# Attention, an expert layer and a routed expert layer in one launch: the second product's last two token groups taken together, later weight splits kept behind the token list, and the places left compared on VectorE

## The chip, the cores and the metric

One core of one Trainium2 chip runs the whole program in one launch. The metric is the device time of that launch in microseconds (us), lower is better. Times of the kernel before are three runs; the trace is one further execution taken with the profiler.

## The reference

The program computes three layers, one behind the other, for 2304 tokens of width 512 (4 sequences of 576 tokens, 8 heads of 64):

```python
x = attention(q, k, v, f)                 # causal, with a decay from cumsum(log f)
h = x @ w_in                              # 512 -> 2048
x = np.maximum(0.01 * h, h) @ w_out       # 2048 -> 512
logits = x @ w_gate                       # 8 experts, cap = 288 tokens for each
for idx in np.argsort(-logits.flatten()): # best pair of token and expert first
    tok, e = idx // 8, idx % 8
    if assigned[tok] < 0 and counts[e] < cap:
        assigned[tok] = e; counts[e] += 1
for e in range(8):
    out[assigned == e] = np.maximum(x[assigned == e] @ w1[e], 0) @ w2[e]   # 512 -> 1024 -> 512
```

Weights of the first two layers come as 64-bit floats. All large products are made from a high and a low part of each operand (fp32r tiles `wh`, `gh`, `gl` and their like): three products for one.

## The kernel before, in words

Four stages follow each other. Attention and the first half of `h` come first, then the second half of `h` with the logits; both are ordered by a planner (`Plan`) that the change does not touch. The stage that the change touches comes next, and the routed experts last.

**The second product** (`x @ w_out`) is a generator, `deferred` (L989). It goes over 9 groups `g` of 256 tokens; for each over two halves of the 2048 inner columns (`half` 0 reads `g1`, which lies in SBUF, `half` 1 reads `gd` from DRAM through the tile `g0`), over four quads `i`, and two blocks `j` of 128 columns. `split_g` (L417) makes `gh` on ScalarE and `gl` on GpSimd. `second` (L425) issues 6 products of 128x512 into the two `acc` tiles of the group and yields behind each one: 96 products for a group, 864 in all. When a group is done, ScalarE copies `acc` to `xo` (two buffers), and SP stores it to `x2d` in DRAM, where the experts' tokens are gathered from.

**The token list** is another generator, `routing` (L1166). It runs 8 phases `ph`, one for each choice of a token that is still free. In 7 of them every expert with too many tokens finds the smallest key that it still takes, by two halves of three steps: VectorE compares all keys with 63 or 31 candidates (`ge`), TensorE counts for each expert and candidate (`q_ct`, 18 small products), VectorE finds how many candidates are exceeded by an expert (`found`), and TensorE turns that into the next `base`. Each count starts with a product of a row of ones (`of`) with minus the places left (`nr`), so that the comparison is with zero. Behind the six steps the counts of the key found go through `q_misc` (products with `on` and with `tru`), and VectorE makes the next phase's choice `oh` and adds the assigned tokens. Behind phase 8 comes the end of the list: a count with `tri`, the position of each token, the tiles `ga`, `oa` (half of it on GpSimd) and three tiles `ob`, 18 products into `q_misc`, and `ids`.

The two are woven by hand: `routing` yields a number of ns where TensorE would wait, and the loop at L1056 then issues products of `deferred` for it, one for each 216 ns of 1.62 times that number. `mm` (L1049) keeps TensorE's order as written. The other engines' orders are made by the tile scheduler from a simulated time, except for instructions issued through the wrappers `vec`, `act`, `gp`, `sp` (`InOrder`, L54), which keep the order of the program among themselves.

**Weights.** All split weights lie in 40 tiles under the tag `w`. In this stage 32 hold the two halves of `w_out` (`wo` and `wo0`, four tiles for each quad). `split_weights` (L317) loads 512 KB into one of two buffers `wst`, and makes two `wh` on ScalarE and two low parts on the engine that it is given: GpSimd for expert 0, VectorE for the others (`fetch`, L1071). Expert 0 takes 32 tiles, 8 of which are free early; the others come free as the last group is done with them.

**Experts.** For each expert, three gathers of 96 tokens on GpSimd (L1088), transposes (`turn`), two layers of products (`first`, `after`) and three scattered stores (`leave`). `fetch(e + 1)` and the gathers of expert `e + 1` are issued before expert `e`'s products.

Of the kernel before, what the change touches and what calls it, by code (L numbers as in the profile page):

```python
# [12 lines left out]
FT = mybir.dt.float32  # L13
FR = mybir.dt.float32r
BF = mybir.dt.bfloat16
I32 = mybir.dt.int32
AF = mybir.ActivationFunctionType
OP = mybir.AluOpType
# [4 lines left out]
E, F2 = 8, 1024  # L23
CAP = NTOK // E
NT = NTOK // 128
GT = 256
# [7 lines left out]
NF = 8  # L34
# [163 lines left out]
def tile_kernel(ctx, tc, q, k, v, f, w_in, w_out, w_gate, w1, w2, out):  # L198
# [218 lines left out]
    def split_g(g):  # L417

        gh = gtp.tile([128, 2, GT], FR, name="gh", tag="gh", bufs=3)
        gl = gtp.tile([128, 2, GT], FR, name="gl", tag="gl", bufs=3)  # L420
        A.copy(gh, g)  # L421
        G.tensor_tensor(gl, g, gh, op=OP.subtract)  # L422
        return gh, gl

    def second(mm, acc, gh, gl, wo, first, last):  # L425
        wh, wl = wo
        for t in range(GT // 128):
            s = slice(128 * t, 128 * t + 128)
            for n, (a, w) in enumerate(((gh, wh), (gh, wl), (gl, wh))):
                mm(acc[t], a[:, s], w, start=first and n == 0, stop=last and n == 2)  # L430
                yield True
# [555 lines left out]


    def deferred(ps, mm):  # L989
        for g in range(NG):  # L990
            acc = [psa.tile([128, 512], FT, name="acc", tag="acc", bufs=ACB) for _ in range(GT // 128)]
            for half in range(2):
                for i in range(NF // 2):
                    if half:
                        x = gtp.tile([128, 2, GT], FT, name="g0", tag="g0", bufs=3)
                        nc.sync.dma_start(x, gd[g][:, 2 * i:2 * i + 2])
                    else:
                        x = g1[g][:, 2 * i:2 * i + 2]
                    gh, gl = split_g(x)
                    for j in range(2):  # L1000
                        w = (wo0 if half else wo)[i]["w"][j]
                        yield from second(mm, acc, gh[:, j], gl[:, j], w, half == i == j == 0, half == j == 1 and i == NF // 2 - 1)
            for t in range(GT // 128):
                xo = gtp.tile([128, DM], FT, name="xo", tag="xo", bufs=2)
                A.copy(xo, acc[t])
                nc.sync.dma_start(x2d[GT * g + 128 * t:GT * g + 128 * t + 128], xo)

    with ExitStack() as c2:
        g1p = c2.enter_context(tc.tile_pool(name="g1", bufs=1, reuse_waits="tile"))
# [43 lines left out]
        wo0 += [{"w": split_weights([(0, 1024, wod[jj])], V)} for jj in range(NF // 4, NF // 2)]  # L1053
        rest = deferred(ps, mm)
        slack = 0
        for ns in routing(nc, rt, ids, ps, W0, mm):  # L1056
            slack += 1.62 * ns
            while slack > 108 and next(rest, None):
                slack -= 216
# [4 lines left out]
    with ExitStack() as c3:  # L1064
# [5 lines left out]

        def fetch(e):  # L1071

            lo_on = G if e == 0 else V
            wa = [[], []]
            for u in range(2):
                for c in range(0, NC, 2):
                    wa[u] += split_weights([(512 * i, 512 * i + 512, w1[e, 128 * (c + i):128 * (c + i) + 128, 512 * u:512 * u + 512])
                                            for i in range(2)], lo_on)
            wb = []
            for j in range(0, NJ, 2):  # L1080
                wb += split_weights([(512 * i, 512 * i + 512, w2[e, 128 * (j + i):128 * (j + i) + 128]) for i in range(2)], lo_on)
            return wa, wb
# [80 lines left out]
            leave(E - 1, ys, t)  # L1163


def routing(nc, wk, ids, ps, W0, mm):  # L1166

# [39 lines left out]
    G.affine_select(tri, on, pattern=[[1, 128]], base=0, channel_multiplier=-1, compare_op=OP.is_gt, fill=0.0)  # L1209
    tru = T("tru", 128, dt=BF)  # L1210
    V.tensor_tensor(tru, on, tri, op=OP.subtract)
    of = T("of", 64)
    G.memset(of, 1.0)
    seg = T("seg", E, NT)
    G.memset(seg, 1.0)
    G.memset(seg[:, :, 0:1], 0.0)
# [19 lines left out]
    for ph in range(E):  # L1236
# [24 lines left out]
        for half in range(2):  # L1261
            base = None
            for n, (K, kt, at0) in enumerate(steps):
                ct = Q("ct", 512, 2)[:, :E]
                mm(ct[:K], of[0:1, :K], nr[0:1], start=True, stop=False)
                ge = T("ge", NT, 63, dt=BF)
                s = [128, NT, K]
                V.scalar_tensor_tensor(ge[:, :, :K], key[:, :, None].to_broadcast(s), base if n else 0.0,
                                       kt[:, None, :].to_broadcast(s), op0=OP.subtract, op1=OP.is_ge)
                yield 500 + 19 * K  # L1270
                for i in range(NT):
                    mm(ct[:K], ge[:, i, :K], oh[:, :, i], start=False, stop=i == NT - 1)
                jk = T("jk", E, dt=BF)
                V.tensor_scalar(jk[at0:at0 + K], ct[:K], 0.0, -1.0, op0=OP.is_ge, op1=OP.max, accum_out=found[at0:at0 + K])
                base = Q("base", 512)[:, 0:1]
                yield 430
                mm(base, unit[:at0 + K], found[:at0 + K], start=True, stop=True)
            yield 480 * (half == 0)
            if half == 0:
                k3 = T("k3", NT)  # L1280
                V.tensor_scalar(k3, key, base, 131072.0, op0=OP.subtract, op1=OP.mult)
                V.tensor_tensor(k3, k3, kf[:, 1], op=OP.add)
                key = k3
# [72 lines left out]
            mm(p[:NB, :2 * NA], ob[:, i - i0, :], oa[:, i].rearrange("p a n -> p (a n)"), start=i == 0, stop=i == NT - 1)  # L1356
    idf = T("idf", NA)
    V.tensor_copy(idf[:NB], p[:NB, NA:2 * NA])
    V.scalar_tensor_tensor(ids, p[:NB, :NA], 128.0, idf[:NB], op0=OP.mult, op1=OP.add)


# [22 lines left out]
```

## Time and profile before

| what | value |
|---|---|
| median of 3 runs | 1039.38 us (1038.36 to 1041.74) |
| the profiled execution | 1040.22 us, its span 1038.5 us |
| mean granted clock of TensorE | 0.982 |
| busy: TensorE / VectorE / ScalarE / GpSimd | 981.7 / 613.5 / 457.3 / 439.4 us |
| second product and token list | about 521 to 798 us |
| experts | about 798 to 1038 us |

The span is from the first to the last instruction in the trace. A line's idle time is that of its engine just before it, with what ended it behind an arrow. A busy TensorE is not TensorE at its peak: products are pipelined, and a record's length overlaps the next record, so prices of products are better read from start to start.

### The profile page before, as it was taken

To read this page: it belongs to the slowest core of one execution; us is meant where nothing else is said; L and a number is where in the kernel's file an instruction comes from. 1 tells how busy PE (TensorE), PEld (TensorE's weight loads), DVE (VectorE), ACT (ScalarE), POOL (GpSimd) and SP (SyncE) were. 2 spreads that over 40 slices of the span, in tenths; PEclk is the share of its full clock that TensorE was granted. 3 is DMA by queue.
4 is the path that set the end of the run, shared out by engine and by line. 5 is a ranking of instruction groups with operands and counts; after the bars stand their busy time and mean duration, and the time that the engine had idled before them with its cause. 6 is when DMAs were issued, how large, how long until landed. Compare 5 with 4: busy or idle time off the path is not lost.

```text
span 1038.5 us, 20151 instructions
## 1 busy us (share of the span) xinstructions
PE 981.7 (95%) x7255; PEld 815.7 (79%) x7255; DVE 613.5 (59%) x1661; ACT 457.3 (44%) x1181; POOL 439.4 (42%) x558
## 2 busy tenths in 40 slices
PE   5999999999989999999999999999985999999996
PEld 3666666777579898889977777777764999999996
DVE  6798998666367787842444445434564565665541
ACT  5798888667523232332412222222141454555531
POOL 6266775322577776700154334444484111222011
PEclk9999999999989999999999999999996999999998
DMA  5577789574498855532221111121134456666521
GB/s 112 139 183 209 209 198 220 147 178 134 123 309 308 265 183 168 145 113 84 86 94 61 43 61 51 62 62 52 51 112 147 145 170 204 195 196 189 161 80 39
DMA packets 145061, 147.67 MB, mean 142 GB/s; under 512 B 70048, under 2 KB 99232, under 8 KB 144704
## 3 DMA queue, kind: packets, MB, share of 16 engines
q1 hardware_dynamic: 141888, 136.93, 45.5%
q0 software_dynamic: 3072, 9.44, 3.1%
q8 instruction: 57, 0.93, 0.4%
q14 instruction: 44, 0.36, 0.1%
HBM read 106.67 MB, written 30.65 MB: 132 GB/s over the span
## 4 chain that ended last, share of the span: by engine, by line
PE 73%; issue 9%; DVE 7%; DMA 5%; POOL 3%; ACT 2%; SPq 0%; POOLq 0%; DVEq 0%
PE acc L1050 20%; PE h L62 19%; PE h L1106 6%; PE y L1119 5%; PE T L62 5%; PE mx L62 5%; PE av L62 5%; PE st L62 3%; PE q_ct L1050 3%; DMA qb<-qa 2%; DMA wst<-in_moe_w 1%; DVE wbits L62 1%; POOL out L1127 1%; DVE kept L62 1%; ACT qa L62 1%
## 5 line engine op out<-in xcount | busy, mean ns | idle before, releaser
L62 PE MATMUL h<-X,wh 128*128 128x256 f32 x1728 | 237.8, 288 | 3.1 <-DVE g L62 3.0
L62 PEld LDWEIGHTS h<-X,wh 128*128 128x128 f32 x1728 | 215.8, 190 | 21.8 <-issue 14.5
L1050 PE MATMUL acc<-wh,gh 128*128 128x512 f32 x576 | 194.6, 406 | 0.0
L422 POOL TENSOR_TENSOR gl<-g,gh 128x512 fp32r<-128x512 f32 x72 | 96.8, 1346 | 128.2 <-ACT gh L421 116.6
L62 ACT ACTIVATE g<-h 128x256 f32<-128x256 f32 x144 | 55.3, 384 | 166.0 <-PE h L62 163.5
L1050 PEld LDWEIGHTS acc<-wh,gh 128*128 128x128 f32 x576 | 109.4, 191 | 20.8
L421 ACT CAST gh<-g 128x512 fp32r<-128x512 f32 x72 | 44.5, 620 | 174.5 <-PE acc L1050 155.4
L1106 PE MATMUL h<-XE,wh 128*128 128x288 f32 x768 | 119.4, 305 | 1.3 <-DVE el L1111 1.0
L1050 PE MATMUL acc<-wh,gl 128*128 128x512 f32 x288 | 119.1, 413 | 0.0
L325 ACT CAST wh<-wst 128x512 fp32r<-128x512 f32 x132 | 79.9, 620 | 85.8 <-DMA wst<-in_moe_w 55.7
L326 DVE TENSOR_TENSOR wh<-wst,wh 128x512 fp32r<-128x512 f32 x116 | 78.2, 688 | 61.7 <-ACT wh L325 53.9
L1106 PEld LDWEIGHTS h<-XE,wh 128*128 128x128 f32 x768 | 107.5, 192 | 2.1 <-DVE el L1111 1.5
L62 ACT ACTIVATE kept<-kept,nm 128x192 f32<-128x192 f32 (+2 forms) x192 | 97.8, 511 | 13.9 <-DVE nm L62 13.8
L62 DVE TENSOR_TENSOR g<-g,h 128x256 f32<-128x256 f32 x144 | 60.1, 417 | 70.4 <-ACT g L62 68.5
L1119 PE MATMUL y<-eh,wh 128*128 128x288 f32 x512 | 98.1, 296 | 0.0
L1119 PEld LDWEIGHTS y<-eh,wh 128*128 128x128 f32 x512 | 79.2, 188 | 0.4 <-ACT eh L1110 0.4
L1127 POOL DMA_INDIRECT out<-yo,ids x24 | 24.2, 1008 | 130.7 <-DVE yo L1126 123.4
L62 DVE CUSTOM_DVE_ANT_0 kept<-mx,mask 128x192 f32<-128x192 f32 (+4 forms) x160 | 63.9, 427 | 21.9 <-PE mx L62 18.0
L62 PE MATMUL mx<-ka,qa 128*128 128x192 f32 (+2 forms) x192 | 68.2, 362 | 5.3 <-DVE nm L62 4.5
L62 PE MATMUL av<-P,vt 128*64 128x256 f32 (+4 forms) x512 | 69.1, 356 | 1.7 <-DVE R L62 1.4
L62 ACT ACTIVATE P<-st 128x320 f32<-128x320 f32 (+2 forms) x128 | 62.9, 500 | 15.7 <-PE st L62 14.8
L62 DVE SCALAR_TENSOR_TENSOR wbits<-w,wbits 128x256 int32<-128x256 int32 x128 | 66.9, 524 | 2.1
(189 smaller groups left out, 1707.2 us busy)
## 6 DMA issues: line engine op xcount, KB each, us to landing
wst<-in_moe_w SPq DMA_DIRECT2D x128, 256.0 KB
X<-xd SPq DMA_DIRECT2D x10, 1024.0 KB
gd<-g SPq DMA_DIRECT2D x36, 256.0 KB
g<-gd SPq DMA_DIRECT2D x36, 256.0 KB
w<-in_moe_w_in SPq DMA_DIRECT2D x32, 256.0 KB
w<-in_moe_w_out SPq DMA_DIRECT2D x32, 256.0 KB
xd<-xt SPq DMA_DIRECT2D x16, 320.0 KB
R<-invd SPq DMA_DIRECT2D x32, 144.0 KB
```

What stands on the lines that cost most here:

```text
L62: r = getattr(self.engine, name)(*a, **k)
L325: A.copy(r[u][0], x)
L326: lo_on.tensor_tensor(r[u][1], x, r[u][0], op=OP.subtract)
L421: A.copy(gh, g)
L422: G.tensor_tensor(gl, g, gh, op=OP.subtract)
L1050: tc.keep_in_program_order(PE.matmul(*a, **k))
L1106: PE.matmul(h[:, :CAP], w, X[:, c, x, :], start=n == 0, stop=n == 3 * NC - 1)
L1119: PE.matmul(yt[c][:, :CAP], w[:, s], a, start=j == 0 and n == 0, stop=j == NJ - 1 and n == 2)
L1127: sd = G.indirect_dma_start(out=out[:, :], out_offset=bass.IndirectOffsetOnAxis(ap=ids[:, 3 * e + t:3 * e + t + 1], axis=0), in_=y, in_off ...
```

## The change

Three edits. In `deferred` groups 7 and 8 are one entry: for each half and quad, the 12 products of group 7 are followed by the 12 of group 8, into four `acc` tiles; their copies and stores come at the end. In `fetch` the low parts of experts 1 to 7, and in `routing` the last operation (`ids`), are issued through `vec`. In the list's steps the product of `of` and `nr` goes; a `tensor_tensor_reduce` adds `nr` to the counts and takes the maximum over the experts, and a comparison of that one column with zero gives `found`.

```diff
     def deferred(ps, mm):
-        for g in range(NG):
-            acc = [psa.tile([128, 512], FT, name="acc", tag="acc", bufs=ACB) for _ in range(GT // 128)]
+        for gs in [[g] for g in range(NG - 2)] + [[NG - 2, NG - 1]]:
+            acc = {g: [psa.tile([128, 512], FT, name="acc", tag="acc", bufs=ACB) for _ in range(GT // 128)] for g in gs}
             for half in range(2):
                 for i in range(NF // 2):
+                    for g in gs:
...
-            for t in range(GT // 128):
+            for g in gs:
+                for t in range(GT // 128):
...
-        for ns in routing(nc, rt, ids, ps, W0, mm):
+        for ns in routing(nc, rt, ids, ps, W0, mm, vec):
...
-            lo_on = G if e == 0 else V
+            lo_on = G if e == 0 else vec
...
-    of = T("of", 64)
-    G.memset(of, 1.0)
...
                 ct = Q("ct", 512, 2)[:, :E]
-                mm(ct[:K], of[0:1, :K], nr[0:1], start=True, stop=False)
...
-                    mm(ct[:K], ge[:, i, :K], oh[:, :, i], start=False, stop=i == NT - 1)
-                jk = T("jk", E, dt=BF)
-                V.tensor_scalar(jk[at0:at0 + K], ct[:K], 0.0, -1.0, op0=OP.is_ge, op1=OP.max, accum_out=found[at0:at0 + K])
+                    mm(ct[:K], ge[:, i, :K], oh[:, :, i], start=i == 0, stop=i == NT - 1)
+                jk, most = T("jk", E), T("most", 1)
+                V.tensor_tensor_reduce(out=jk[:K], in0=ct[:K], in1=nr[:K], scale=1.0, scalar=-3e38, op0=OP.add, op1=OP.max, accum_out=most[:K])
+                V.tensor_scalar(found[at0:at0 + K], most[:K], 0.0, None, op0=OP.is_ge)
...
-    V.scalar_tensor_tensor(ids, p[:NB, :NA], 128.0, idf[:NB], op0=OP.mult, op1=OP.add)
+    vec.scalar_tensor_tensor(ids, p[:NB, :NA], 128.0, idf[:NB], op0=OP.mult, op1=OP.add)
```

How instructions move. On TensorE, behind the first step of a half, before (`q_base` is the new base, `acc` the second product):

```order
L1050 MATMUL q_base<-r_found,r_unit 128x1
L1050 MATMUL q_ct<-r_nr,r_of 31x8
L1050 MATMUL acc<-wh,gl 128x512
L1050 MATMUL acc<-wh,gh 128x512 x2
L1050 MATMUL acc<-wh,gl 128x512
```

and with the change:

```order
L1053 MATMUL q_base<-r_found,r_unit 128x1
L1053 MATMUL acc<-wh,gl 128x512
L1053 MATMUL acc<-wh,gh 128x512 x2
L1053 MATMUL acc<-wh,gl 128x512
```

The product of `nr` and `of` is gone, and the products of the second layer close up.

On VectorE at the end of the list, before (`wh<-wst,wh` is the low part of a weight of expert 1; the T rows belong to the transposes of expert 0's tokens):

```order
L1345 TENSOR_TENSOR r_ga<-r_na,r_io 128x432
L1353 TENSOR_TENSOR r_ob<-r_nb,r_io 128x576
L1348 TENSOR_TENSOR r_oa<-r_ga,r_it 128x18x24
L326 TENSOR_TENSOR wh<-wst,wh 128x512 x2
L1353 TENSOR_TENSOR r_ob<-r_nb,r_io 128x576
L326 TENSOR_TENSOR wh<-wst,wh 128x512
L1353 TENSOR_TENSOR r_ob<-r_nb,r_io 128x576
L326 TENSOR_TENSOR wh<-wst,wh 128x512
L1358 COPY r_idf<-q_misc 96x24
L1359 SCALAR_TENSOR_TENSOR ids<-q_misc,r_idf 96x24
L1098 TENSOR_TENSOR XE<-T_9963,XE 128x288
```

and with the change:

```order
L1346 TENSOR_TENSOR r_ga<-r_na,r_io 128x432
L1354 TENSOR_TENSOR r_ob<-r_nb,r_io 128x576
L1349 TENSOR_TENSOR r_oa<-r_ga,r_it 128x18x24
L1354 TENSOR_TENSOR r_ob<-r_nb,r_io 128x576 x2
L1359 COPY r_idf<-q_misc 96x24
L62 SCALAR_TENSOR_TENSOR ids<-q_misc,r_idf 96x24
L1101 TENSOR_TENSOR XE<-T_10003,XE 128x288
L1101 TENSOR_TENSOR XE<-T_10009,XE 128x288
L1101 TENSOR_TENSOR XE<-T_10015,XE 128x288
L1101 TENSOR_TENSOR XE<-T_10021,XE 128x288
L62 TENSOR_TENSOR wh<-wst,wh 128x512 x4
```

The four splits stand behind `ids` and the four low parts of expert 0's tokens.

On GpSimd from the first weights of groups 7 and 8 (`g_7`, `g_8`), before (`gl` is the low part of the second product's other operand):

```order
L422 TENSOR_TENSOR gl<-g_7_5396,gh 128x512 x4
L1314 TENSOR_SCALAR r_nr<-r_rp 128x8
L1315 TENSOR_SCALAR r_r<-r_rp 128x8
L422 TENSOR_TENSOR gl<-g_9362,gh 128x512
L1316 TENSOR_TENSOR r_nr<-r_nr,r_r 128x8
L1313 TENSOR_TENSOR r_A<-r_A,r_asg 128x144
L422 TENSOR_TENSOR gl<-g_9402,gh 128x512
L422 TENSOR_TENSOR gl<-g_9446,gh 128x512
L422 TENSOR_TENSOR gl<-g_9490,gh 128x512
L422 TENSOR_TENSOR gl<-g_8_5397,gh 128x512 x3
L326 TENSOR_TENSOR wh<-wst,wh 128x512
```

and with the change:

```order
L422 TENSOR_TENSOR gl<-g_7_5396,gh 128x512
L422 TENSOR_TENSOR gl<-g_8_5397,gh 128x512
L422 TENSOR_TENSOR gl<-g_7_5396,gh 128x512
L422 TENSOR_TENSOR gl<-g_8_5397,gh 128x512
L326 TENSOR_TENSOR wh<-wst,wh 128x512
L1315 TENSOR_SCALAR r_nr<-r_rp 128x8
L1316 TENSOR_SCALAR r_r<-r_rp 128x8
L422 TENSOR_TENSOR gl<-g_7_5396,gh 128x512
L1317 TENSOR_TENSOR r_nr<-r_nr,r_r 128x8
L326 TENSOR_TENSOR wh<-wst,wh 128x512
L1314 TENSOR_TENSOR r_A<-r_A,r_asg 128x144
L422 TENSOR_TENSOR gl<-g_8_5397,gh 128x512
```

The first of expert 0's twelve late splits stood behind eleven `gl` of the two groups; now it stands behind four, and the others follow one by one between the `gl`.

## Rows read from the trace of the kernel before

**Rows 1.** Busy time in stretches: stretch, its length, PE, PEld, DVE, ACT, POOL, clock, DMA.

```profile
680.00:720.00 40.00, 40.00 (x286) 29.33 (x285) 16.89 (x50) 7.82 (x13) 17.26 (x16) 1.00 0.22 60
...
830.00:860.00 30.00, 30.00 (x234) 29.98 (x233) 17.46 (x33) 15.23 (x32) 6.28 (x6) 1.00 0.60 184
```

**Rows 2.** Waits, 520 to 770 us: total us, times, longest.

```profile
PE q_misc L1050 <- DVE r_rs L1288: 1.7, 3, 1.2
```

**Rows 3.** Timeline of TensorE, end of the list: start, us, instruction, idle before.

```profile
768.90 0.18 PE L1050 MATMUL q_misc<-r_rs,r_tru 128*128 128x8 bf16 x1
...
780.26 0.17 PE L1050 MATMUL q_misc<-r_rs,r_tri 128*128 128x8 bf16 x1 [4.25 <-DVE r_rs L1323]
...
786.75 0.41 PE L1050 MATMUL q_misc<-r_oa,r_ob 128*96 128x48 bf16 x6
...
798.28 1.29 PE L1096 MATMUL T<-ident,xe 96*128 96x96 f32 x4 [4.74 <-DMA xe<-x2d,ids]
```

**Rows 4.** Timeline of VectorE, end of the list.

```profile
771.38 1.39 DVE L1240 TENSOR_TENSOR r_eq<-r_W,r_m 128x144 f32<-128x144 f32 x1
...
787.40 0.69 DVE L326 TENSOR_TENSOR wh<-wst,wh 128x512 fp32r<-128x512 f32 x1 [2.57 <-ACT wh L325]
...
789.02 0.75 DVE L1353 TENSOR_TENSOR r_ob<-r_nb,r_io 128x576 bf16<-128x576 f32 x1
791.45 0.69 DVE L326 TENSOR_TENSOR wh<-wst,wh 128x512 fp32r<-128x512 f32 x1 [1.68 <-ACT wh L325]
...
793.79 0.18 DVE L1359 SCALAR_TENSOR_TENSOR ids<-q_misc,r_idf 96x24 int32<-96x24 f32 x1
```

**Rows 5.** Timeline of GpSimd, end of the list.

```profile
776.01 4.99 POOL L326 TENSOR_TENSOR wh<-wst,wh 128x512 fp32r<-128x512 f32 x4
783.75 2.25 POOL L1347 TENSOR_SCALAR r_oa<-r_ga,r_ip 128x432 bf16<-128x432 bf16 x1 [2.74 <-DVE r_ga L1345]
794.27 1.17 POOL L1088 DMA_INDIRECT xe<-x2d,ids  x1 [8.27 <-DVE ids L1359]
```

**Rows 6.** Instructions by line and shape, 520 to 800 us: count, busy us, mean ns, idle.

```profile
L1050 PE MATMUL q_ct<-r_nr,r_of 1*31 1x8 f32 x56 | 6.2, 180 | 0.0
```

**Rows 7.** Timeline of TensorE, steps of the search.

```profile
747.90 0.18 PE L1050 MATMUL q_base<-r_found,r_unit 95*128 95x1 bf16 x1
...
748.49 0.63 PE L1050 MATMUL acc<-wh,gh 128*128 128x512 f32 x2
...
751.58 0.18 PE L1050 MATMUL q_base<-r_found,r_unit 127*128 127x1 bf16 x1
...
751.94 0.39 PE L1050 MATMUL acc<-wh,gl 128*128 128x512 f32 x1
752.17 0.63 PE L1050 MATMUL acc<-wh,gh 128*128 128x512 f32 x2
...
753.27 0.63 PE L1050 MATMUL acc<-wh,gh 128*128 128x512 f32 x2
```

**Rows 8.** Timeline of VectorE: one step's count, and a short operation inside SBUF.

```profile
750.88 0.16 DVE L1274 TENSOR_SCALAR_CACHE_REDUCE r_jk<-q_ct 31x8 bf16<-31x8 f32 x1 [1.95 <-PE q_ct L1050]
750.97 0.08 DVE L1274 DVE_READ_ACCUMULATOR r_jk<-q_ct 31x1 bf16 x1
...
782.74 0.18 DVE L1337 TENSOR_SCALAR r_na<-r_na 128x18 f32<-128x18 f32 x1
```

**Rows 9.** Instructions of VectorE by line and shape, whole span.

```profile
L62 DVE CUSTOM_DVE_ANT_0 kept<-mx,mask 128x64 f32<-128x64 f32 x32 | 7.0, 219 | 0.0
...
L1300 DVE TENSOR_SCALAR r_pen<-r_rp 128x8 f32<-128x8 f32 x7 | 2.9, 410 | 0.2
```

**Rows 10.** Timeline of TensorE, one phase earlier.

```profile
732.90 0.18 PE L1050 MATMUL q_misc<-r_rs,r_tru 128*128 128x8 bf16 x1
```

**Rows 11.** Timeline of VectorE, one phase earlier.

```profile
735.37 0.30 DVE L1240 TENSOR_TENSOR r_eq<-r_W,r_m 128x144 f32<-128x144 f32 x1
...
739.63 1.39 DVE L1246 TENSOR_TENSOR r_oh<-r_mw,r_we 128x144 bf16<-128x144 f32 x1
```

More of the change, by code (lines that the diff above doesn't have):

```diff
@@ L989, in deferred @@
     def deferred(ps, mm):
-        for g in range(NG):
-            acc = [psa.tile([128, 512], FT, name="acc", tag="acc", bufs=ACB) for _ in range(GT // 128)]
+        for gs in [[g] for g in range(NG - 2)] + [[NG - 2, NG - 1]]:
+            acc = {g: [psa.tile([128, 512], FT, name="acc", tag="acc", bufs=ACB) for _ in range(GT // 128)] for g in gs}
             for half in range(2):
                 for i in range(NF // 2):
[L994 to L1002, printed above, removed]
-            for t in range(GT // 128):
-                xo = gtp.tile([128, DM], FT, name="xo", tag="xo", bufs=2)
-                A.copy(xo, acc[t])
-                nc.sync.dma_start(x2d[GT * g + 128 * t:GT * g + 128 * t + 128], xo)
+                    for g in gs:
+                        if half:
+                            x = gtp.tile([128, 2, GT], FT, name="g0", tag="g0", bufs=3)
+                            nc.sync.dma_start(x, gd[g][:, 2 * i:2 * i + 2])
+                        else:
+                            x = g1[g][:, 2 * i:2 * i + 2]
+                        gh, gl = split_g(x)
+                        for j in range(2):
+                            w = (wo0 if half else wo)[i]["w"][j]
+                            yield from second(mm, acc[g], gh[:, j], gl[:, j], w, half == i == j == 0, half == j == 1 and i == NF // 2 - 1)
+            for g in gs:
+                for t in range(GT // 128):
+                    xo = gtp.tile([128, DM], FT, name="xo", tag="xo", bufs=2)
+                    A.copy(xo, acc[g][t])
+                    nc.sync.dma_start(x2d[GT * g + 128 * t:GT * g + 128 * t + 128], xo)
     with ExitStack() as c2:
@@ L1163, in tile_kernel, with routing @@
             leave(E - 1, ys, t)
-def routing(nc, wk, ids, ps, W0, mm):
+def routing(nc, wk, ids, ps, W0, mm, vec):
     V, G = nc.vector, nc.gpsimd
```

## The prediction

> **What bounds the kernel now.** I read the stretches first, to find the stage that the change touches and what fills it. While the second product and the token list run together (about 521 to 776 us), TensorE is busy in all of a 40 us stretch at full granted clock; in the expert stage likewise [rows 1]. So in both stages time goes down only if TensorE has less to do. Next, the waits: up to 770 us TensorE stands still for VectorE's counts for only 1.7 us in all [rows 2]. Then the timelines of the end of the list, engine by engine, because there the picture turns. The reader should follow the product with `tru` at 768.90, the one with `tri` at 780.26 behind a 4.25 us wait for VectorE, the 22 products of the second product behind it (up to 786.5), and the gathered tokens only at 798.28 [rows 3]. On VectorE `eq` takes 1.39 us, where one phase earlier it takes 0.30 [rows 4, 11], two weight splits of expert 1 stand ahead of the second and the third `ob`, and `ids` ends at 793.97 (793.79 and 0.18) [rows 4]. On GpSimd four weight splits of expert 0 run back to back there, and the first gather starts 0.3 us behind `ids` [rows 5]. So 768.90 to 798.28 is a chain of VectorE, not of TensorE.
>
> **Places left compared on VectorE.** Removed: 42 small fp32 products (`nr` by `of`), each two passes (28 of them are the 56 passes in [rows 6]). Their price is read from start to start, since records overlap. From `q_base` to the second `acc` row behind it took 748.49 - 747.90 = 0.59 us with such a product and 751.94 - 751.58 = 0.36 without [rows 7]: 0.23 us, 28 times, 6.4 us. The other 14 open a half: 752.17 to 753.27 is 1.10 us for three `acc` products (two at 752.17, the third's row is left out), which at 0.23 each (751.94 to 752.17) need 0.69: 0.41 us, 14 times, 5.7 us. Together 12.1 us of an engine with no idle time. Some repeats show up to 0.32 for the first kind, so 14.5 is the upper bound; what stands behind the removed product is `acc` work in the same order, so I take all 12.1.
>
> Added on VectorE per step: the reduction changes its form (the custom operation on 64 columns took 0.22 us, so 8 columns take at most that [rows 9], 0.06 more than the 0.16 removed [rows 8]), and there is one more comparison on a single column, taken as 0.18 from `na` [rows 8]. The accumulator read ended at 751.05 and `q_base` started at 751.58 [rows 7, 8]; this 0.53 us is the tightest of the 42, and `acc` products fill it. So the addition is free, with about 0.3 us left. If that cover goes, it is by GpSimd: `pen`, also a short comparison inside SBUF, has a mean of 0.41 [rows 9] instead of some 0.18, that is holds of about 1.1 us in one case of five. By that row some 8 of the 42 would overrun the cover by 0.8 us: up to +7 us. I take 0, since one column is less than anything that was held, and keep 7 for the range. A page of the Trainium skill says why the row may not apply: "VectorE: DVE Perf Modes", section "Mode 2×_2P — use both read ports for one tensor", wants an outermost dimension longer than one, which a single column does not have; by it the sum has 0 here, by `pen` 7. No run so far shows a one-column case.
>
> **The last two groups together.** TensorE gets the same 192 products in another order. What changes is when weights come free: a quad of `w` tiles is released after 24 products of the pair, the first some 22 us (96 products at 0.23) earlier than in the old order, where only group 8 released them. GpSimd's 12 splits of expert 0 therefore move from the last 25 us (four at 776.01 [rows 5]) to the last phase and a half, about one behind each `gl` (the GpSimd rows of the section on the change). Two effects.
>
> (a) Behind `tru` GpSimd has two splits and two `gl` left, instead of six and two, the last of them before `tri`. The path from `tru` to `tri` took 11.36 us [rows 3]. The same path one phase earlier, `tru` at 732.90 to the end of `oh` at 741.02, took 8.1 with only `gl` beside it [rows 10, 11]; that one has the keys and a `ge` more, and `As` and `rs` less. The floor is the 30 `acc` products between the two, 6.9 us. I take 8.0: 3.3 us less (0 to 4.4).
>
> (b) The price: per 24 products of the pair GpSimd now has two `gl` and two splits, 5 us at 1.25 [rows 5], instead of 2.5. VectorE's held operations multiply there. The last phase of before had some of this and cost TensorE 1.2 us [rows 2]. I charge +2 us (0 to 5). This is the rule that speaks against the change: the Trainium skill, "GPSIMD Engine Reference", section "1. Specifications", says that GpSimd shares its SBUF interfaces with VectorE and contends with instructions that have two SBUF inputs or run in a two-port mode. The trace agrees (1.39 against 0.30 us [rows 4, 11]).
>
> Stores: the last four `x2d` stores now leave together through two `xo` buffers, behind two weight loads on SP's queue, whose buffers are free by then. `ids` will end some 4 us behind the last product (below), which leaves room for two copies and their stores, so the gathers should not see them (0 to +1).
>
> **Later splits behind the list.** Between `tri` and the end of `ids` lay 13.71 us [rows 3, 4]. Now nothing of expert 1 stands in it. First `misc` product: 22 `acc` products at 0.23 are 5.1 us, GpSimd's `oa` ended 5.74 behind `tri` [rows 5] with a held scan ahead of it; I take 5.5 instead of 6.49. Then three blocks of products at 0.41 [rows 3], two `ob` at 0.75 between them, `idf` and `ids` at 0.18 [rows 4], and six hand-overs of about 0.06: 3.5 us. Together 9.0: 4.7 us less (3 to 5). What was waited for there, four splits, comes behind the four `XE` of expert 0, while TensorE works on expert 0; expert 1 needs them some 20 us later. For experts 2 to 7 three splits each slide behind the `ys` copies: VectorE has room, and TensorE is full at 30.00 of 30 us [rows 1], so 0, bounded by +6.
>
> **Sum.** -12.1 - 3.3 - 4.7 + 2 = -18.1 us. The profiled execution took 1040.22 (its span is 1038.5), which gives 1022.1; it lies 0.84 above the median of 1039.38, so 1021.3.
>
> **Rivals.**
> 1. *VectorE held by GpSimd becomes the bound.* The comparison is held like `pen` (+7), the pair costs 5, and the tail gains the same: -12.1 - 8 + 12 = -8, 1031. For it: the holds are in the trace. Against: the cover of 0.3 us and more at every step. 0.15.
> 2. *The tail falls to TensorE's floor* and the holds cost nothing: -12.1 - 4.4 - 5 = -21.5, about 1018, or with the dearer removed products (-14.5) 1015.5. For it: VectorE's free operations are short. Against: two splits and two `gl` remain there. 0.10.
> 3. *The expert stage gives it back.* The stage starts earlier, but weights come later: three splits of 0.69 us [rows 4] behind the copies at six boundaries, half of it uncovered: +6, about 1027; more if loads queue behind them. Against: TensorE full. 0.10.
> 4. *TensorE runs dry in the pair* (slower). GpSimd works in order, and `gl` of the next weights stands behind a split that waits for ScalarE's cast, which waits for tiles that TensorE has just released. The path, release to `gl`, is two casts and two operations of GpSimd at 1.25 us [rows 5], an estimated 4 us, against 24 products at 0.23, 5.5 us. It decides from 5.5 us on; to eat 18.1 us at six releases it must take 8.5, and anything above gives over 1039; at 9.5 it is 1045. 0.04.
> 5. *The list was not bound by TensorE*, so that removed products leave only gaps, and the tail moves its wait to the stores: 1037 to 1040. Against: 40.00 of 40 us busy. 0.04.
>
> **Numbers.** My own case (about 1018 to 1027) has 0.57. Range 1013 to 1034: it takes in rivals 1 to 3 and the ends of the unknown costs. Within 0.3% (3 us), about what a measurement of this kernel can tell, lies rival 5 and a thin part of rival 1: 0.06. Slower: rival 4 with a rest, 0.05. Faster: 0.89.
>
> **What would show it.** Each phase, from `tru` to `tru`, should be 1.7 us shorter (four times 0.23 and two times 0.41). VectorE's new comparison should take 0.2 us everywhere; a mean above 0.4 is rival 1, and TensorE's waits for `found` would show it. The wait ahead of `tri` should fall from 4.25 to about 1 us, `ids` should come about 17 us behind `tru`, with no split between `ga` and `ids`, and the first gather 0.3 us behind it. If gathers wait for `x2d`, the stores are late. If the expert stage is longer than the 240 us behind 798.28, rival 3. A gain under 5 us, or TensorE waiting for `gl` in the pair, would prove me wrong.

## The result, and the profile after

The changed kernel took **1022.56 us** (median of 4 runs, 1021.77 to 1029.56), the kernel before 1040.56 beside it (4 runs). The ratio is 0.984, 95% interval 0.9805 to 0.9875: some 18 us less. The profiled execution took 1021.89, its span is 1020.2, so 18.3 less than the span before.

The same stretches of the second product and of the experts, moved along by what was gained (stretch, its length, PE, PEld, DVE, ACT, POOL, clock, DMA), answer to [rows 1]:

```profile
664.00:704.00 40.00, 40.00 (x283) 29.73 (x282) 18.16 (x56) 8.45 (x14) 18.20 (x17) 1.00 0.21 60
812.00:842.00 30.00, 30.00 (x234) 29.98 (x233) 18.07 (x34) 14.76 (x31) 6.72 (x6) 1.00 0.59 190
```

TensorE is as full as before. The new comparison, VectorE's instructions by line and shape (count, busy us, mean ns, idle):

```profile
L1275 DVE TENSOR_SCALAR r_found<-r_most 31x1 bf16<-31x1 f32 x28 | 4.1, 148 | 1.0
L1301 DVE TENSOR_SCALAR r_pen<-r_rp 128x8 f32<-128x8 f32 x7 | 3.9, 555 | 0.2
...
L1275 DVE TENSOR_SCALAR r_found<-r_most 63x1 bf16<-63x1 f32 x14 | 2.1, 149 | 0.5
```

All 42 took 0.15 us, and 21 of them began while GpSimd was in the middle of a `gl` or of a split: none was held, while `pen`, eight columns wide, rose from a mean of 410 ns [rows 9] to 555. TensorE's waits from 520 to 755 us (total, times, longest) show no wait for `found`, but a new one:

```profile
PE q_ct L1053 <- DVE r_oh L1247: 2.1, 1, 2.1
```

The end of the list on TensorE (start, us, instruction, idle before), against [rows 3]:

```profile
761.37 0.18 PE L1053 MATMUL q_misc<-r_rs,r_tru 128*128 128x8 bf16 x1
769.66 0.17 PE L1053 MATMUL q_misc<-r_rs,r_tri 128*128 128x8 bf16 x1 [1.20 <-DVE r_rs L1324]
774.76 0.41 PE L1053 MATMUL q_misc<-r_oa,r_ob 128*96 128x48 bf16 x6
...
782.01 0.56 PE L1099 MATMUL T<-ident,xe 96*128 96x96 f32 x2 [4.25 <-DMA xe<-x2d,ids]
```

and on VectorE, against [rows 4]:

```profile
772.89 0.60 DVE L1349 TENSOR_TENSOR r_oa<-r_ga,r_it 128x432 bf16<-128x432 bf16 x1
775.21 0.76 DVE L1354 TENSOR_TENSOR r_ob<-r_nb,r_io 128x576 bf16<-128x576 f32 x1 [1.71 <-PE q_misc L1053]
776.51 0.76 DVE L1354 TENSOR_TENSOR r_ob<-r_nb,r_io 128x576 bf16<-128x576 f32 x1 [0.54 <-PE q_misc L1053]
...
778.02 0.18 DVE L62 SCALAR_TENSOR_TENSOR ids<-q_misc,r_idf 96x24 int32<-96x24 f32 x1
```

No split stands there now; VectorE waits for TensorE's products instead. `ids` ends at 778.20, 16.8 us behind `tru` (25.07 before; about 17 was forecast).

**Where the time went.** The total hides it, because the stages ahead of this one, which no edit touches, ended anywhere from 515.7 to 524.8 us in the fourteen profiled executions of this study. So I cut every execution at the same marks on TensorE and VectorE: the first product `acc` with `sel` (the stage begins), the seven `tru` (five phases lie between the first six), `tri`, the end of `ids`, the first `T` behind it, and the end of the last engine instruction. All in us:

| execution | to 1st tru | five phases | last phase | tru to tri | tri to ids | ids to T | T to end | sum |
|---|---|---|---|---|---|---|---|---|
| before | 40.1 | 174.3 | 36.0 | 11.4 | 13.7 | 4.3 | 235.4 | 515.2 |
| after | 40.1 | 166.4 | 36.8 | 8.3 | 8.5 | 3.8 | 233.4 | 497.3 |
| cmp_only | 40.1 | 166.4 | 33.5 | 12.5 | 14.8 | 4.2 | 235.3 | 506.7 |
| pair_only | 40.0 | 174.3 | 37.9 | 8.3 | 10.0 | 4.1 | 234.2 | 508.8 |
| behind_only | 41.7 | 174.3 | 36.0 | 11.4 | 9.9 | 6.2 | 233.7 | 513.2 |
| start_twice | 42.2 | 176.9 | 36.4 | 11.4 | 13.7 | 4.3 | 234.5 | 519.4 |
| start_apart | 42.4 | 185.8 | 37.0 | 12.4 | 14.8 | 3.7 | 236.7 | 532.9 |
| pair_behind | 41.7 | 174.3 | 36.4 | 8.3 | 8.5 | 3.7 | 234.2 | 507.1 |
| cmp_behind | 40.0 | 166.4 | 33.5 | 12.4 | 10.5 | 6.5 | 233.7 | 503.0 |
| three_more | 39.4 | 171.5 | 37.7 | 8.3 | 8.6 | 3.8 | 234.2 | 503.5 |
| eight_wide | 42.0 | 170.6 | 39.0 | 8.3 | 8.6 | 3.8 | 233.8 | 506.2 |
| split0_dve | 40.0 | 166.4 | 33.1 | 7.4 | 8.6 | 3.8 | 233.6 | 492.8 |
| three_ob | 38.5 | 166.4 | 36.7 | 8.3 | 7.0 | 5.3 | 234.2 | 496.4 |
| together | 38.5 | 166.4 | 33.1 | 7.4 | 7.0 | 5.4 | 233.3 | 491.0 |

The first column holds a surprise: the first phase, with six removed products, did not get shorter. The granted clock says why. The first 15 us of the stage, before and then after (the clock is the third number from the end):

```profile
518.57:533.57 15.00, 15.00 (x100) 11.89 (x97) 7.43 (x22) 2.45 (x5) 11.14 (x24) 0.89 0.34 117
```

```profile
518.12:533.12 15.00, 15.00 (x84) 12.42 (x81) 5.51 (x22) 2.45 (x5) 9.85 (x23) 0.77 0.36 116
```

In each of the fourteen executions this clock was 0.89 or 0.77. At 0.89 the first column reads 40.1 and 40.0 with the old comparison (before, pair_only), 38.5 with the new one (three_ob, together); at 0.77 41.7 (behind_only, pair_behind) and 40.0 to 40.1 (after, cmp_only, cmp_behind, split0_dve). So the first phase did gain 1.6 us, and a lower clock at the border of the stage, which comes with the old comparison and with the new, took it back in this execution: 1.6 us between executions of the same comparison, (0.89 - 0.77) x 15 = 1.8 us by the clock.

The last phase grew instead of shrinking. TensorE and VectorE there:

```profile
735.83 0.73 PE L1053 MATMUL q_ct<-r_oh,r_ge 128*63 128x8 bf16 x18 [2.09 <-DVE r_oh L1247]
...
737.97 1.06 PE L1053 MATMUL acc<-wh,gh 128*128 128x512 f32 x2
738.83 0.63 PE L1053 MATMUL acc<-wh,gl 128*128 128x512 f32 x1
```

```profile
732.00 1.24 DVE L1245 TENSOR_TENSOR r_mw<-r_mw,r_U 128x18 f32<-128x18 f32 x1
733.16 1.33 DVE L1268 SCALAR_TENSOR_TENSOR r_ge<-r_kf,r_step 128x1134 bf16<-128x1134 f32 x1
734.41 1.36 DVE L1247 TENSOR_TENSOR r_oh<-r_mw,r_we 128x144 bf16<-128x144 f32 x1
```

`mw` takes 1.24 us (0.17 in split0_dve, below), `oh` 1.36, TensorE stands still 2.09 us, and then a second price falls due: from 737.97 to 738.83 two products of 512 columns took 0.43 us each where they take 0.23 [rows 7]. The granted clock after that wait, in 3 us (the third number from the end):

```profile
737.00:740.00 3.00, 3.00 (x9) 2.16 (x9) 0.86 (x2) 0.62 (x1) 1.27 (x1) 0.60 0.41 154
```

So most of it is at the lower of the clock's two levels, 1.2 GHz. Before, the 4.25 us wait ahead of `tri` [rows 3] was followed by the same, and behind the 1.20 us that are left of it now it is not (before, then after):

```profile
780.00:784.00 4.00, 3.74 (x11) 3.02 (x11) 3.79 (x11) 0.00 (x0) 1.26 (x2) 0.60 0.32 109
```

```profile
768.00:772.00 4.00, 2.80 (x14) 2.12 (x13) 3.58 (x14) 0.44 (x1) 0.34 (x1) 1.00 0.32 112
```

### The profile page after: what moved, and what is told of

Its sections match the earlier page's. It is cut to its first block, busy times and chain, and to the rows that moved or that the text cites. A ratio compares the mean times of both kernels' runs of the same rounds, so it can differ in the third digit from the quotient of the medians.

```text
span 1020.2 us, 20022 instructions
## 1 busy us (share of the span) xinstructions
PE 968.5 (95%) x7171; PEld 807.9 (79%) x7171; DVE 615.3 (60%) x1703; ACT 457.9 (45%) x1181; POOL 443.0 (43%) x557
## 4 chain that ended last, share of the span: by engine, by line
PE 75%; issue 9%; DVE 6%; DMA 4%; ACT 3%; POOL 2%; POOLq 0%; SPq 0%; DVEq 0%; ACTq 0%
PE h L62 19%; PE acc L1053 19%; PE h L1109 6%; PE y L1122 6%; PE T L62 5%; PE mx L62 5%; PE av L62 5%; PE st L62 4%; PE q_ct L1053 3%; DMA qb<-qa 2%; ACT qa L62 1%; POOL out L1130 1%; DMA X<-xd 1%; DVE qa L62 1%; DVE wh L62 1%
## 5 line engine op out<-in xcount | busy, mean ns | idle before, releaser
L1053 PE MATMUL acc<-wh,gh 128*128 128x512 f32 x576 | 191.0, 405 | 0.0
L62 DVE TENSOR_TENSOR wh<-wst,wh 128x512 fp32r<-128x512 f32 x132 | 90.3, 704 | 40.1 <-ACT wh L325 29.8
```

What stands on the lines that cost most here:

```text
L62: r = getattr(self.engine, name)(*a, **k)
L1053: tc.keep_in_program_order(PE.matmul(*a, **k))
```

## The experiments

The kernel before, measured beside these runs, took 1041.97 us (start_twice, cmp_only, pair_only, behind_only), 1043.57 (start_apart, pair_behind, cmp_behind, three_more), 1042.67 (split0_dve, three_ob, eight_wide) and 1040.0 (together); ratios are to those, with their 95% intervals. A phase below is one of the middle ones of the five, `tru` to `tru`.

**The price of the removed product.** start_twice adds, to the kernel before, a second product behind each one that the change removes:

```diff
                 mm(ct[:K], of[0:1, :K], nr[0:1], start=True, stop=False)
+                mm(ct[:K], of[0:1, :K], zr[0:1], start=False, stop=False)
```

> The kernel before with each count's starting product issued twice, the second with a row of zeros: it doubles the cost that the change removes. Theory (TensorE bounds the search): full phases grow from 34.7 to about 36.3 us, the time by 11 to 13 us, to about 1052. Rival (the search is bound by VectorE's chain and the removed products lay in slack): phases stay near 34.7, time at 1040 to 1042.

1043.23 us, ratio 1.0018 (0.9991 to 1.0045), which the total can't tell from the kernel before; the phases can. They went from 34.69 to 35.20: 0.085 us for each product added, a third of what I took for a removed one. The size was missed; TensorE's rows (start, us) show why:

```profile
747.34 0.17 PE L1050 MATMUL q_base<-r_found,r_unit 63*128 63x1 bf16 x1
747.44 0.22 PE L1050 MATMUL q_ct<-r_nr,r_of 1*31 1x8 f32 x2
747.52 0.20 PE L1050 MATMUL q_ct<-r_zr,r_of 1*31 1x8 f32 x2
747.65 0.50 PE L1050 MATMUL acc<-wh,gl 128*128 128x512 f32 x1
```

The second stands 0.08 behind the first. Perhaps what is dear is not the product but the place between small and large ones. start_apart therefore puts the added product alone among the large ones:

```diff
-                yield 500 + 19 * K
+                yield 250 + 9.5 * K
+                mm(ct[:K], of[0:1, :K], zr[0:1], start=False, stop=False)
+                yield 250 + 9.5 * K
```

> The kernel before with one more small product per step, of ones with a row of zeros, standing alone in the middle of the second product's rows instead of behind the removed product's place. Theory (a small product costs TensorE what it takes to interrupt the rows of 512, some 0.27 us, and only 0.085 us where another small one stands next to it): the full phases grow by 6 times 0.2 to 0.3 us, from 34.7 to 36.0 to 36.4, and the time by 8 to 13 us, to about 1050. Rival (each such product costs its own 0.085 us wherever it stands, and the removed one was dearer for another reason): phases 35.2, as with the product doubled, time 1043.

1061.54 us, ratio 1.0176 (1.013 to 1.0222), phases of 37.0: 0.39 us each, more than either theory said. TensorE's rows there:

```profile
747.12 0.40 PE L1050 MATMUL acc<-wh,gl 128*128 128x512 f32 x1
747.44 0.22 PE L1050 MATMUL q_ct<-r_zr,r_of 1*31 1x8 f32 x2
747.60 0.73 PE L1050 MATMUL acc<-wh,gh 128*128 128x512 f32 x2
748.16 0.39 PE L1050 MATMUL acc<-wh,gl 128*128 128x512 f32 x1
```

From the large product ahead to the second `gl` it took 1.04 us, where three large ones take 0.69. The removed product gave 0.27 in the mean of a phase, (34.69 - 33.08) / 6. The mean hides three kinds of place: cut at the same instructions of one phase, before and after, the six gave 0.42, 0.17, 0.23, 0.40, 0.15 and 0.24 us. The two dear ones open a half and stand between large products, as the added one of start_apart does. The other four stand behind `q_base`, the cheaper of them behind the first step of a half (before, then after: 0.59 us from `q_base` to the second `acc` row, then 0.44):

```profile
639.52 0.17 PE L1050 MATMUL q_base<-r_found,r_unit 63*128 63x1 bf16 x1
...
640.11 0.63 PE L1050 MATMUL acc<-wh,gh 128*128 128x512 f32 x2
```

```profile
635.57 0.17 PE L1053 MATMUL q_base<-r_found,r_unit 63*128 63x1 bf16 x1
...
636.01 0.62 PE L1053 MATMUL acc<-wh,gh 128*128 128x512 f32 x2
```

Behind the second step it is 0.36 with the change, the figure that [rows 7] have without such a product. So two passes cost 0.085, 0.15 to 0.24, or 0.39 to 0.42 us by what stands on either side. That TensorE bounds the search holds: every addition lengthened it.

**Each edit alone.** cmp_only has the comparison alone (the part of the diff that changes the list's steps).

> The kernel before with the comparison alone changed: the product of nr and of is gone, VectorE compares. Theory (TensorE bounds the search, the new comparison is covered): each full phase, tru to tru, falls from 34.7 to 33.1 us, the last phase stays near 36.0 less 1.6, tru to tri stays near 11.4 and tri to ids near 13.7, and the time falls by 11 to 12 us, to about 1028.5. Rival (the list is not bound by TensorE): phases stay at 34.7 and the time at 1040. Rival (the comparison is held like pen): found comes late at some steps, phases differ, the time falls by only about 5 us, to 1035.

1031.14 us, ratio 0.9898 (0.9866 to 0.9931). Phases 33.07 to 33.08, as forecast; but `tru` to `tri` and `tri` to `ids` each grew by 1.1, which no theory had. On GpSimd four splits still stand at the end (767.02 x4), and TensorE's wait ahead of `tri` rose from 4.25 to 5.4 us: without the pair a faster search waits longer for the same tail. The other 1.1 us goes with the clock, which in the 6 us from `tri` on was 0.59, against 0.75 before: 0.16 x 6 = 1.0. pair_only has the pair alone:

> The kernel before with the last two groups together, nothing else. Theory: tru to tri falls from 11.4 to about 8.3 us, the last phase grows from 36.0 to about 38.4 (GpSimd's splits beside VectorE's list), the end of the list keeps most of its length since two splits of expert 1 still stand ahead of the second and third ob; together -1 to -3 us, about 1038. Rival (the pair costs nothing in the last phase): -4 us or more, 1036 or less. Rival (the pair loses more than the tail gives): slower, 1042 or more.

1034.27 us, ratio 0.9941 (0.9905 to 0.9977): better than I said, by the tail. The total is that of the first rival, the pieces are not: the last phase grew to 37.9. `tri` to `ids` fell from 13.7 to 10.0 although splits of expert 1 stayed in it (VectorE, then TensorE's first product with `oa`, 6.1 us behind `tri`):

```profile
784.13 1.03 DVE L326 TENSOR_TENSOR wh<-wst,wh 128x512 fp32r<-128x512 f32 x1
785.88 0.76 DVE L1356 TENSOR_TENSOR r_ob<-r_nb,r_io 128x576 bf16<-128x576 f32 x1 [0.71 <-PE q_misc L1053]
786.56 0.69 DVE L326 TENSOR_TENSOR wh<-wst,wh 128x512 fp32r<-128x512 f32 x1
787.37 0.76 DVE L1356 TENSOR_TENSOR r_ob<-r_nb,r_io 128x576 bf16<-128x576 f32 x1
```

```profile
785.43 0.41 PE L1053 MATMUL q_misc<-r_oa,r_ob 128*96 128x48 bf16 x6 [0.85 <-POOL r_oa L1350]
```

Neither of these splits waits for ScalarE's cast, as two did before for 2.57 and 1.68 us [rows 4]; so from that first product to the end of `ids` it is 3.9 us, where it was 7.2 (786.75 to 793.97 [rows 3, 4]). Behind the first split VectorE still waits 0.71 us for TensorE, so they cost little: without them, but with the pair (pair_behind below), `tri` to `ids` is 8.5, 1.5 less. behind_only has the order of the splits and of `ids` alone (`vec` for `V` in `fetch` and at `ids`):

> The kernel before with only the order of the later experts' splits and of ids changed. Theory: tri to ids falls from 13.7 us to 9 to 10 (no split between ga and ids, but four splits of GpSimd still beside them), phases stay at 34.7, tru to tri at 11.4; the stretch from ids to the end gets shorter by up to 2.5 us if the expert stage's gain seen in the full change comes from this edit, and stays at 244.5 if not. Time: -4 to -5 us without that (1035.5), -6 to -7 with it (1033.5). Rival (expert 1's weights come late and the expert stage gives it back): 1040.

1038.68 us, ratio 0.9973 (0.9948 to 0.9999). `tri` to `ids` is 9.9, as forecast, 6.5 us up to the first product with `oa` as before and 3.4 behind it; but the first gather then waits for the stores of the second product (GpSimd):

```profile
798.96 1.17 POOL L1088 DMA_INDIRECT xe<-x2d,ids  x1 [7.05 <-DMA x2d<-xo]
```

so 1.9 of the 3.8 us were lost again (`ids` to T 6.2).

**Each edit taken out.** pair_behind is the changed kernel with `nr` times `of` back:

> The changed kernel with the old comparison (the product of nr and of is back). Theory (the parts add up): full phases 34.7, the last phase 37.9 as with the pair alone, tru to tri 8.3, tri to ids 8.5; 7.9 and 1.1 us more than the changed kernel, about 1031.5. Rival (the pair and the order of the splits already bring all that the tail gives, and the comparison's gain is absorbed elsewhere): within 3 us of the changed kernel.

1031.9 us, ratio 0.9905 (0.9862 to 0.9948): phases 34.7 as the theory has it, though the last one was 36.4, not 37.9. The clock makes the difference. In pair_only and here TensorE has the same instructions in that phase and the same wait of 1.68 us for `oh`; the 3 us from 1.2 us behind the start of the product that waited, in pair_only and then here:

```profile
745.60:748.60 3.00, 3.00 (x10) 2.10 (x9) 0.81 (x1) 0.62 (x1) 1.27 (x1) 0.53 0.47 163
```

```profile
744.10:747.10 3.00, 3.00 (x26) 2.00 (x25) 0.80 (x1) 1.28 (x3) 1.29 (x1) 1.00 0.46 152
```

So the lower clock is worth 1.4 us there, and the same wait is not followed by it in every execution. cmp_behind is the changed kernel without the pair:

> The changed kernel without the pair. Theory: phases 33.1, the last one 33.5 (3.2 less than with the pair), tru to tri 12.4, tri to ids 10 to 11, since GpSimd's splits pile up behind the last group again, and the first gather waits for the x2d stores (ids to the first transpose 6 us instead of 3.8): -3.2 + 4.1 + 2 + 2.2, about 5 us more than the changed kernel, 1027.5. Rival (GpSimd's splits cost the tail nothing once VectorE's are gone): 1020 to 1022.

1027.46 us, ratio 0.9862 (0.9822 to 0.9902): the theory's number, and its pieces (33.5, 12.4, 10.5, 6.5).

**How much cover the new comparison has.** three_more lengthens the chain by three one-column operations:

```diff
+                for _ in range(3):
+                    m2 = T("most2", 1, bufs=2)
+                    V.tensor_scalar(m2[:K], most[:K], 1.0, None, op0=OP.mult)
+                    most = m2
                 V.tensor_scalar(found[at0:at0 + K], most[:K], 0.0, None, op0=OP.is_ge)
```

> The changed kernel with three more one-column operations of VectorE, one behind the other, between the reduction and the comparison of each step, some 0.2 us each. Theory (the search has 0.33 to 0.58 us of cover left between found and q_base): 0.6 us more overrun it by 0.05 to 0.3 at each of 42 steps, 2 to 12 us more, about 1030, and TensorE's waits for found appear. Rival (no cover, VectorE's chain is the bound): +25 us, 1048. Rival (one-column operations are held by GpSimd like pen): more than that. Rival (free, cover far larger than the rows say): 1022.5.

1027.47 us, ratio 0.9859 (0.9824 to 0.9893), 5 us over the changed kernel. The six phases grew by 6.0 us, 0.17 for a step, for a chain 0.54 longer (one step on VectorE):

```profile
604.23 0.51 DVE L1277 TENSOR_SCALAR r_most<-r_most 63x1 f32<-63x1 f32 x3
604.77 0.15 DVE L1279 TENSOR_SCALAR r_found<-r_most 63x1 bf16<-63x1 f32 x1
```

So 0.37 us was left in the mean, with the steps spread from no overrun at all to 0.28 us, and the one operation that the change adds was free. Of these 168 one-column operations none took over 0.15. eight_wide puts one of eight columns there, and a maximum behind it:

```diff
+                m8, most = T("m8", E), T("most2", 1)
+                V.tensor_scalar(m8[:K], jk[:K], 1.0, None, op0=OP.mult)
+                V.tensor_reduce(most[:K], m8[:K], axis=AX.X, op=OP.max)
                 V.tensor_scalar(found[at0:at0 + K], most[:K], 0.0, None, op0=OP.is_ge)
```

> The changed kernel with two more operations in each step's chain: a copy of the 8 columns of jk inside SBUF (63x8 or 31x8) and a maximum over them, ahead of the comparison. Theory (one column is never held, eight are, as pen is): the 8-column operation takes 0.17 us alone and 1 us or more beside GpSimd's work, a mean of 0.4 or more, and each hold is a wait of TensorE of up to 1 us: 42 steps, a fifth to two fifths held, +8 to +18 us, 1030 to 1040. Rival (short operations are not held for their width but for where they stand, and here none is): 0.17 each, with the maximum 0.4 us more in the chain, 0 to +4 us, 1023 to 1026.

1032.86 us, ratio 0.99 (0.9862 to 0.9939). VectorE by line and shape:

```profile
L1276 DVE TENSOR_SCALAR r_m<-r_jk 31x8 f32<-31x8 f32 x28 | 10.3, 369 | 1.0
...
L1276 DVE TENSOR_SCALAR r_m<-r_jk 63x8 f32<-63x8 f32 x14 | 3.8, 268 | 0.5
```

27 of the 42 took 0.16 or 0.17 us, the others 0.36 to 1.06, and TensorE waited 13 times for `found` (5.8 us). The mean of 0.34 is below the 0.4 I named, but at the same place eight columns are held and one is not. All 15 long ones began beside a `gl` or a split of GpSimd and ended 0.02 us behind it, like the longest:

```profile
618.04 1.29 POOL L422 TENSOR_TENSOR gl<-g,gh 128x512 fp32r<-128x512 f32 x1 [3.10 <-ACT gh L421]
618.29 1.06 DVE L1276 TENSOR_SCALAR r_m<-r_jk 31x8 f32<-31x8 f32 x1
```

Of the 27 short ones 22 began with no such operation under way, and five some 0.10 us ahead of its end.

**What the pair costs.** split0_dve takes GpSimd's splits away from the list (`lo_on = V if e == 0 else vec`):

> The changed kernel with expert 0's low parts on VectorE instead of GpSimd, in the scheduler's order. Theory (the pair costs the last phase 3.7 us because GpSimd's splits hold VectorE's list): GpSimd has only gl there, VectorE's 128x144 operations are held less, the 2.1 us wait for oh goes and the last phase falls from 36.8 towards 33.5; but twelve splits of 0.69 us stand in VectorE's own queue, so the gain is 1 to 3 us, about 1020.5. Rival (VectorE's own splits cost the list as much as the holds): 1022 to 1025, last phase 36 to 38, with TensorE waiting for VectorE behind a split. Rival (the last phase is long for another reason, weights or gh): last phase stays 36.8 and the wait is for something else.

1021.43 us, ratio 0.9789 (0.975 to 0.9829). The last phase is 33.1, `tru` to `tri` 7.4, the wait for `oh` is gone. VectorE at the place where TensorE waited for it:

```profile
734.06 0.17 DVE L1245 TENSOR_TENSOR r_mw<-r_mw,r_U 128x18 f32<-128x18 f32 x1
...
735.44 1.40 DVE L1247 TENSOR_TENSOR r_oh<-r_mw,r_we 128x144 bf16<-128x144 f32 x1
```

`oh` still takes 1.40 us there, beside a `gl`, but `mw` is short. The clock stays at 1.00 from 730 to 750 us:

```profile
730.00:750.00 20.00, 20.00 (x133) 15.23 (x131) 15.21 (x36) 7.15 (x12) 9.51 (x9) 1.00 0.32 105
```

So the pair's 3.7 us were GpSimd's holds and what followed from them, not the order of TensorE's products, which is the same in both, instruction by instruction: 2.15 us were lost up to the product that waits for `oh`, and nearly all of the rest, 1.4, in the seven `acc` products at the lower clock. The whole from the stage's start is 4.5 us less (497.3 to 492.8, both at a clock of 0.77). The totals don't show it well: the two profiled executions differ by 0.25 us, because the stages ahead ended 3.9 us later in this one, and the ratios, 0.9789 and 0.984, have intervals that overlap. three_ob gives `ob` three buffers (`ob = T("ob", 6, NB, dt=BF, bufs=3)`):

> The changed kernel with three buffers for ob, so that VectorE makes the second and third ob without waiting for q_misc. Theory: VectorE's waits of 1.71 and 0.54 us and TensorE's two of 0.85 go, but oa's half on VectorE comes later; tri to ids falls from 8.5 to about 7.0, and the time by 1 to 1.5 us, to about 1021. Rival (the first gather waits for x2d stores instead): ids earlier, the first transpose not, 1022.5. Rival (oa on VectorE is late): tri to ids as before or longer.

1023.65 us, ratio 0.9847 (0.9804 to 0.989): `ids` 1.5 us earlier, `ids` to T 1.5 longer. The rival was right, the gather waits for the stores:

```profile
776.65 1.17 POOL L1091 DMA_INDIRECT xe<-x2d,ids  x1 [3.73 <-DMA x2d<-xo]
```

together has both, and takes `g0` buffers for the last two copies:

```diff
+                    if g == NG - 1:
+                        xo = gtp.tile([128, 2, GT], FT, name="g0", tag="g0", bufs=3).rearrange("p a b -> p (a b)")
+                    else:
+                        xo = gtp.tile([128, DM], FT, name="xo", tag="xo", bufs=2)
```

> The changed kernel with three edits: expert 0's low parts on VectorE, three buffers for ob, and the last two copies of the second product into g0 buffers instead of waiting for the two xo buffers. Theory (each removes a wait that was seen): the last phase 33.1 and tru to tri 7.4 as with the first edit alone, tri to ids 7.0 as with three buffers, ids to the first transpose 3.8 again since the x2d stores leave some 1.5 us earlier; -3.7 - 0.9 - 1.5, from the start of the stage to the end 6 us less than the changed kernel, about 1017. Rival (the stores still end last): the first transpose only where the first edit alone has it, 1.5 us later, 1018.5. Rival (VectorE's splits end up in the tail when the order shifts): 1021.

**1015.77 us** (1015.11 to 1017.36), ratio 0.9762 (0.9737 to 0.9787), faster than the changed kernel by intervals that do not meet; split0_dve's interval overlaps with it. From the stage's start it is 1.8 us better than split0_dve, and 1.6 of that is the clock of the first 15 us (0.89 against 0.77); the other two edits brought nothing clear. ScalarE's rows say why the new buffers didn't help:

```profile
768.04 1.26 ACT L1011 COPY g<-acc 128x512 f32<-128x512 f32 x2 [1.51 <-PE acc L1056]
```

The last copies wait for the last products, not for a buffer; the time from `tri` to the first T is 12.4 us here as in split0_dve.

## Why the prediction was right, step by step

The forecast of 1021.3 came out 1.3 us below the median; beside the kernel before that was measured with it, the gain is 18.0 us for 18.1. So close a sum is partly luck. Its main terms hold to within 1 us, but four errors on one side (removed products 1.0 less, `tru` to `tri` 0.2 less, the pair 0.4 dearer, 1.6 lost to the clock at the border of the stage) met three on the other (`tri` to `ids` 0.5 more, the gathers 0.5 and the experts 2.1, both put at nothing).

- **The removed products**, 1.74 us a phase, 12.1 in all: measured 1.57 in the mean of the five phases and 1.6 in the first once the clock is taken out, so some 11.1. The term that was mis-sized is the 0.23 taken for all 28 products behind `q_base`: half of them gave 0.23 to 0.24, the half behind the first step only 0.15 to 0.17. The 0.41 for the 14 that open a half was right (0.40 and 0.42). I had read both from one example each.
- **The new comparison**: free, as said, with 0.37 us left in the mean (said: 0.3). One column was never held, eight columns were, in 15 of 42. This fits what the Trainium skill's "VectorE: DVE Perf Modes", section "Mode 2×_2P — use both read ports for one tensor", states of the outermost dimension, and which the prediction set against the row of `pen`. That the mode is the reason is not shown; that one column escapes is. Rival 1's first half falls by it.
- **(a) `tru` to `tri`**: 8.3 us for 8.0; it comes with the pair alone.
- **(b) the pair's price**, +2 (0 to 5): the last phase is 3.7 over a clean one against 1.3 before, 2.4 net. Against the same kernel without the pair (cmp_behind, 33.5) it is 3.2. The mechanism was as argued, but not whole: some 2.1 us are the wait for `oh`, and 1.4 of the rest the lower clock behind it, which I had not counted.
- **`tri` to `ids`**, 13.71 to 9.0: measured 8.5. Two pieces make it. Up to the first product with `oa` it fell from 6.5 to 5.1 (said: 5.5), because with the shorter wait ahead of `tri` the clock stayed up (0.60 against 1.00): the pair brings that (pair_behind), though alone it leaves 6.1, since TensorE then waits 0.85 us for GpSimd's half of `oa`; the order of the splits alone leaves 6.5 (behind_only). Behind that product it fell from 7.2 to 3.4 (said: 3.5), and here either edit would do: the order takes the splits out, and with the pair alone they no longer wait for their casts (3.9). So the two take 3.8 and 3.7 off alone and 5.2 together. Without the pair half of what the order brings is lost to the stores. I had called those a risk of the pair.
- **The experts**, 0: 2.1 us less in this execution. About half is the clock, 0.63 before and 0.72 after in the 12 us from the first T on: 0.09 x 12 = 1.1. The rest is the order of the splits. Before, TensorE waited twice for VectorE's `el` (the low part of an expert's hidden layer) from 805 us on (total, times, longest); the second time that `el` stood behind two splits that had waited for ScalarE's cast (VectorE):

```profile
PE h L1106 <- DVE el L1111: 1.0, 2, 0.6
```

```profile
890.33 1.52 DVE L326 TENSOR_TENSOR wh<-wst,wh 128x512 fp32r<-128x512 f32 x2 [3.77 <-ACT wh L325]
891.77 0.45 DVE L1111 SCALAR_TENSOR_TENSOR el<-h,eh 128x288 fp32r<-128x288 f32 x1
```

In each of the five executions with the old order TensorE waits for `el` in this stage, 0.6 to 2.1 us in all; in the nine with the new one no such wait is listed. Rival 3 is excluded: the order that I had put at nothing brings about 1 us.
- **Rivals 2, 4 and 5**: `tru` to `tri` is 1.4 us above the floor of 6.9; TensorE's list of waits has none for weights or `gl` in the pair; and the phases got shorter, so the search was bound by TensorE.

From the sum of the rows, start of the stage to end, the 17.9 us are: five phases 7.9, first phase 0 (1.6 less 1.6 of clock), last phase -0.8, `tru` to `tri` 3.1, `tri` to `ids` 5.2, gathers 0.5, experts 2.1.

## What to carry to other kernels

Price a wait of the matrix engine with what comes behind it: the wait of 2.1 us for `oh` cost 3.7, because the products behind it ran at the lower clock, and one of 1.7 us cost 3.2 in an execution where the clock fell (pair_only) and 1.7 in one where it did not (pair_behind). Before an operation of VectorE goes into a tight chain beside GpSimd, look at its width as well as at its length, and make it one column if it can be. And cut executions at marks of the program: the totals moved by several us for reasons outside the change, while a phase repeated to 0.02 us.

## What the runs showed that I had not expected

- A product of two small passes cost TensorE 0.085 us behind another small one, 0.15 to 0.24 behind `q_base`, and 0.39 to 0.42 alone among large ones.
- The granted clock at the border of the stage, behind a row of small products, was 0.89 or 0.77 over 15 us in each execution, worth 1.6 us. What draws it is open; the edits don't, since both values occur with and without each.
- VectorE doing the twelve splits in its own queue (some 0.7 us each, three of them 1.2 to 1.4) disturbed the list less than GpSimd doing them beside it: the last phase is 33.1 us against 36.8.
